# One ring and one DMA queue for K, V and weights, and identity matmuls in place of an add tree, in a decode step

## The chip, the cores and the metric

The kernel runs on one core of one Trainium2 chip. The metric is the time of one execution on the device in microseconds (us). The kernel before takes 1370.1 us (median of 3 runs, 1369.82 to 1370.17). All times named "span" run from the first to the last instruction of a profiled execution and are about 2 to 3 us shorter than the measured time.

## The reference, cut to what matters

One token (a row x of 640 values) goes through attention over a cache and through a gated FFN. The results and x are added up.

```python
xn = layernorm(x)                                   # 1 x 640
q  = xn @ wq                                        # 32 heads x 128
scores = einsum("hd,hkd->hk", q, k_cache) * 128**-0.5   # 32 heads, 32768 keys
p  = softmax(scores)
o  = einsum("hk,hkd->hd", p, v_cache)
y  = x + o.reshape(4096) @ wo + (silu(xn @ w_gate) * (xn @ w_up)) @ w_down
```

The K cache and the V cache have 32 heads x 32768 keys x 128 values in bf16, 268 MB each. With the weights some 555 MB have to come from HBM. One head has 16.78 MB of K and V.

## The kernel before

K lies in SBUF with 128 keys on the partitions and the 128 values of a key along the free axis. So the dot product with q is a multiply and a sum along the free axis, and both are VectorE's. V needs no such work: TensorE takes blocks of V as stationary operand and a column of p as moving operand (the PV matmuls, below).

K has its own ring of four slots of 2 MB, loaded from SyncE's queue. V has another ring of four, loaded from ScalarE's queue. A head has four K chunks. VectorE's loop, cut:

```python
for i in range(NKC):                  # NKC = 128 chunks of 2 MB
    h, c = divmod(i, NCK)             # NCK = 4 chunks per head
    ...
    v.wait_ge(kdma[slot].sem, ...)    # chunk landed
    dve_t.inc(v.tensor_tensor(out=kr, in0=kr, in1=qbh, op=ALU.mult))
    for w in [64, 32, 16, 8]:         # the add tree, in place
        dve_t.inc(v.tensor_tensor(out=kr[:, :, 0:w], in0=kr[:, :, 0:w],
                                  in1=kr[:, :, w:2 * w], op=ALU.add))
    v3 = dve_t.inc(v.tensor_reduce(out=scs[...], in_=kr[:, :, 0:8], axis=AX.X, op=ALU.add))
    ...
    if c == NCK - 1:
        head_ops(h)                   # max over the free axis: pmax
        if h >= 1:
            rz_op(h - 1)              # waits for GpSimd's sum of head h-1, then 1/sum
```

GpSimd joins the partitions, and ScalarE makes the exp between GpSimd's two steps:

```python
for b in range(H):                                  # GpSimd
    wait(pmax of b);  partition_all_reduce(gmaxb, pmax, max)
    tensor_scalar(negb = -scale * gmaxb)            # ScalarE: exp waits for this
    wait(exp of b);   partition_all_reduce(zb, rowsum, add)   # rz_op waits for this
```

Of the kernel before, what the change touches and what calls it, by code (L numbers as in the profile page):

```python
# [5 lines left out]
ALU = mybir.AluOpType  # L7
# [4 lines left out]


class Ctr:

    def __init__(self, sem, step=1):
        self.sem = sem
        self.step = step
        self.n = 0

    def inc(self, ins):
        ins.then_inc(self.sem, self.step)
        self.n += self.step
        return self.n


def bass_parallel_sum__gqa_block_cached__swiglu_ffn__decode_kernel(
# [16 lines left out]
    HQ = A_wq.shape[1] // DH  # L44
    F = B_w_gate.shape[1]
    assert DH == 128 and HQ == H, (DH, HQ, H)
    assert D % 128 == 0
    NC_D = D // 128
    NJ = SK // 128
    assert SK % 128 == 0  # L50
    CKK = 64 if NJ >= 64 else NJ
    CKV = 64 if NJ >= 64 else NJ
    assert NJ % CKK == 0 and NJ % CKV == 0
    NCK = NJ // CKK
    NCV = NJ // CKV
    NKC = NCK * H
    NVC = NCV * H
    KR = 4
    VR = 4
    PR = 3  # L60
    SCR = 3
    SR = 4
    TREE = [64, 32, 16, 8]
    NLVL = 2 + len(TREE)
    c_scale = float(DH) ** -0.5
    eps = 1e-5
    FB = (F + 127) // 128
    F_LAST = F - (FB - 1) * 128
    DB = 2
    DBW = D // DB  # L70
    QB = min(512, HQ * DH)
    NQB = (HQ * DH) // QB
    assert D % DB == 0 and DBW <= 512 and (HQ * DH) % QB == 0

    VPK = NCV // NCK
    order = []
    emitted_v = set()

    def _emit_v(q):
        if 0 <= q < NVC and q not in emitted_v:  # L80
            order.append(("v", q))
            emitted_v.add(q)

    for i in range(NKC):
        order.append(("k", i))
        h = i // NCK
        ci = i % NCK
        for vv in range(VPK):
            _emit_v((h - 1) * NCV + ci * VPK + vv)
    for q in range(NVC):  # L90
        _emit_v(q)
    assert CKV == CKK, "V-in-K-slot staging needs equal chunk sizes"
    LASTV_Q0 = (H - 1) * NCV

    def v_buf(q):
        return ("v", q % VR, None)
    WO_POS = min(KR - 1, NKC - 1)
    FFNW_POS = min(1, NKC - 1)

    with ExitStack() as es:  # L100
# [5 lines left out]

        krings = sbt("krings", [128, KR, CKK * DH], BF16)
        vrings = sbt("vrings", [128, VR, CKV * DH], BF16)
        WQO = max(NC_D * HQ * DH, H * D)
        wqo = sbt("wqo", [128, WQO], BF16)  # L110
        qb = sbt("qb", [128, HQ * DH], BF16)
        xnb = sbt("xnb", [128, NC_D, 128], BF16)
        sc = sbt("sc", [128, SCR, NJ], F32)
        P = sbt("P", [128, PR, NJ], BF16)
        ocol = sbt("ocol", [128, HQ], BF16)
        xncol = sbt("xncol", [128, NC_D], BF16)
        hcol = sbt("hcol", [128, FB], BF16)
        sg = sbt("sg", [128, FB], F32)
        pmax = sbt("pmax", [128, SR], F32)
        gmaxb = sbt("gmaxb", [128, SR], F32)  # L120
        negb = sbt("negb", [128, SR], F32)
        rowsum = sbt("rowsum", [128, SR], F32)
        zb = sbt("zb", [128, SR], F32)
        rzb = sbt("rzb", [128, SR], F32)
        xrowb = sbt("xrowb", [1, D], BF16)
        rows = sbt("rows", [1, 4, D], F32)
        outb = sbt("outb", [1, D], BF16)
        st = sbt("st", [1, 8], F32)
        one1 = sbt("one1", [1, 2], F32)
        s_x = sem("c_x")  # L130
        s_wq = sem("c_wq")
        s_ffn = sem("c_ffn")
        s_wo = sem("c_wo")
        s_out = sem("c_out")
        kd_sems = [sem(f"kd{i}") for i in range(KR)]
        vd_sems = [sem(f"vd{i}") for i in range(VR)]
        s_pe_a = sem("pe_a")
        s_pe_pv = sem("pe_pv")
        s_pe_c = sem("pe_c")
        s_dve_a = sem("dve_a")  # L140
        s_dve_t = sem("dve_t")
        s_dve_max = sem("dve_max")
        s_dve_rz = sem("dve_rz")
        s_dve_c = sem("dve_c")
        s_act_a = sem("act_a")
        s_act_exp = sem("act_exp")
        s_act_ov = sem("act_ov")
        s_pool_a = sem("pool_a")
        s_pool_g = sem("pool_g")
        s_pool_neg = sem("pool_neg")  # L150
        s_pool_z = sem("pool_z")
        block = es.enter_context(nc.Block())

        c_x = Ctr(s_x, 16)
        c_wq = Ctr(s_wq, 16)
        c_ffn = Ctr(s_ffn, 16)
        c_wo = Ctr(s_wo, 16)
        c_out = Ctr(s_out, 16)
        kdma = [Ctr(s, 16) for s in kd_sems]
        vdma = [Ctr(s, 16) for s in vd_sems]  # L160
        pe_a = Ctr(s_pe_a)
        pe_pv = Ctr(s_pe_pv)
        pe_c = Ctr(s_pe_c)
        dve_a = Ctr(s_dve_a)
        dve_t = Ctr(s_dve_t)
        dve_max = Ctr(s_dve_max)
        dve_rz = Ctr(s_dve_rz)
        dve_c = Ctr(s_dve_c)
        act_a = Ctr(s_act_a)
        act_exp = Ctr(s_act_exp)  # L170
        act_ov = Ctr(s_act_ov)
        pool_a = Ctr(s_pool_a)
        pool_g = Ctr(s_pool_g)
        pool_neg = Ctr(s_pool_neg)
        pool_z = Ctr(s_pool_z)

        kflat = krings[:, :, :].rearrange("p s n -> p (s n)")
        vflat = vrings[:, :, :].rearrange("p s n -> p (s n)")
        wq_v = wqo[:, 0:NC_D * HQ * DH].rearrange("p (c n) -> p c n", c=NC_D)
        wo_v = wqo[:, 0:H * D].rearrange("p (h n) -> p h n", h=H)  # L180
        assert 2 * NC_D * F + FB * D <= VR * CKV * DH, "V ring too small to host FFN weights"
        wg_sb = vflat[:, 0:NC_D * F].rearrange("p (c n) -> p c n", c=NC_D)
        wu_sb = vflat[:, NC_D * F:2 * NC_D * F].rearrange("p (c n) -> p c n", c=NC_D)
        wd_sb = vflat[:, 2 * NC_D * F:2 * NC_D * F + FB * D].rearrange("p (j d) -> p j d", j=FB)
        VSLOTS_FFN = ((2 * NC_D * F + FB * D) * 2 + CKV * DH * 2 - 1) // (CKV * DH * 2)
        xf = rows[0:1, 0, :]
        xc = rows[0:1, 1, :]
        xnrow = rows[0:1, 2, :]
        ffnrow = rows[0:1, 3, :]
        mile = {}  # L190

        with nc.psum_tensor("ps8", [128, 8, 512], F32) as ps8:
            psA = ps8[:, 0, :]
            psG = ps8[:, 1, :]
            psF = ps8[0:1, 2:2 + DB, :]
            psR = ps8[0:1, 4:6, :]
            O = [ps8[:, 6, :], ps8[:, 7, :]]
            QPS = [ps8[:, b, 0:QB] for b in range(8)]
            assert NQB <= 8

            @block.vector
            def dve_phase_a(v):
                dve_a.inc(v.memset(one1[0:1, :], 1.0))
                v.wait_ge(c_x.sem, 16)
                dve_a.inc(v.tensor_copy(out=xf, in_=xrowb[0:1, :]))
                v.wait_ge(dve_a.sem, dve_a.n)
                dve_a.inc(v.tensor_reduce(out=st[0:1, 0:1], in_=xf, axis=AX.X, op=ALU.add))
                v.wait_ge(dve_a.sem, dve_a.n)
                dve_a.inc(v.tensor_scalar(out=st[0:1, 1:2], in0=st[0:1, 0:1], scalar1=1.0 / D,
                                          scalar2=None, op0=ALU.mult))  # L210
                v.wait_ge(dve_a.sem, dve_a.n)
                dve_a.inc(v.tensor_scalar(out=xc, in0=xf, scalar1=st[0:1, 1:2], scalar2=None,
                                          op0=ALU.subtract))
                v.wait_ge(dve_a.sem, dve_a.n)
                dve_a.inc(v.tensor_tensor_reduce(out=xnrow, in0=xc, in1=xc, scale=1.0, scalar=0.0,
                                                 op0=ALU.mult, op1=ALU.add, accum_out=st[0:1, 2:3]))
                v.wait_ge(dve_a.sem, dve_a.n)
                mile["ve"] = dve_a.inc(v.tensor_scalar(out=st[0:1, 3:4], in0=st[0:1, 2:3], scalar1=1.0 / D,
                                                       scalar2=eps, op0=ALU.mult, op1=ALU.add))

            @block.scalar
            def act_phase_a(a):
                a.wait_ge(dve_a.sem, mile["ve"])
                mile["sqrt"] = act_a.inc(a.activation(out=st[0:1, 4:5], in_=st[0:1, 3:4], func=ACTF.Sqrt))

            @block.vector
            def dve_phase_a2(v):
                v.wait_ge(act_a.sem, mile["sqrt"])
                dve_a.inc(v.reciprocal(out=st[0:1, 5:6], in_=st[0:1, 4:5]))
                v.wait_ge(dve_a.sem, dve_a.n)  # L230
                mile["xnrow"] = dve_a.inc(v.tensor_scalar(out=xnrow, in0=xc, scalar1=st[0:1, 5:6],
                                                          scalar2=None, op0=ALU.mult))
# [104 lines left out]
            def dve_phase_b(v):  # L337
# [14 lines left out]
                for i in range(NKC):  # L352
# [4 lines left out]
                    if c == 0 and h >= SCR:  # L357
                        v.wait_ge(act_exp.sem, h - SCR + 1)
# [195 lines left out]
```

## Time and profile before

| | |
|---|---|
| span | 1367.0 us |
| VectorE busy | 1263.9 us, 92% |
| bytes moved | 555.19 MB, 406 GB/s over the span |
| VectorE per 2 MB of K | 9.82 us from chunk to chunk |
| from one head's max to the next (mean of heads 4 to 29) | 39.80 us |

First come lines of the page of the kernel before: the busy time of the engines, then three rows of 40 equal slices of the span (busy tenths of VectorE, busy tenths of the DMA engines, GB/s), then the chain that ended last, by engine.

```profile
PE 272.6 (20%) x8474; PEld 240.2 (18%) x8474; DVE 1263.9 (92%) x859; ACT 31.9 (2%) x102; POOL 201.3 (15%) x100
...
DVE  5907999999999999999999999999999999999994
...
DMA  9999599999999999999999999999999999999994
GB/s 389 401 415 381 214 424 388 419 419 415 416 426 418 427 418 422 424 419 426 418 421 420 424 420 423 427 420 425 422 421 424 417 427 425 419 426 427 414 381 183
...
DVE 90%; another core or an unknown queue 3%; issue 2%; SPq 2%; DMA 1%; PE 1%; POOL 0%; ACT 0%; POOLq 0%
```

VectorE is full except at the start and the end, and it is the chain. But the DMA row is full as well, at 414 to 427 GB/s from the eighth slice to the third from the end. The fifth slice moves only 214 GB/s and the last only 183.

The groups of instructions by shape say what a chunk costs VectorE (count, then busy us and mean ns of one, then idle time before them):

```profile
L361 DVE TENSOR_TENSOR krings<-krings,qb 128x8192 bf16<-128x8192 bf16 x128 | 564.9, 4413 | 43.5 <-DMA krings<-in_A_k_cache_dram 43.5
L365 DVE TENSOR_TENSOR krings<-krings 128x4096 bf16<-128x4096 bf16 x128 | 293.3, 2292 | 4.4
...
L365 DVE TENSOR_TENSOR krings<-krings 128x2048 bf16<-128x2048 bf16 x128 | 156.8, 1225 | 4.4
...
L365 DVE TENSOR_TENSOR krings<-krings 128x1024 bf16<-128x1024 bf16 x128 | 88.5, 691 | 4.4
L368 DVE TENSOR_REDUCE sc<-krings 128x64 f32<-128x512 bf16 x128 | 87.8, 686 | 4.4
L365 DVE TENSOR_TENSOR krings<-krings 128x512 bf16<-128x512 bf16 x128 | 54.3, 424 | 4.4
```

The multiply takes 4.41 us and the four steps of the tree 2.29, 1.23, 0.69 and 0.42 us, together 4.63 us.

### The profile page before, as it was taken

Reading aid. Unit: us, or ns where it says so; the run is one execution under the profiler, and the core shown is the slowest. Engines: PE = TensorE matmul, PEld = TensorE weight load, DVE = VectorE, ACT = ScalarE, POOL = GpSimd, SP = SyncE. Lnnn points to the kernel's source line nnn. Section 1 sums busy time; section 2 is a strip of 40 time slices with the busy share of each in tenths; the row PEclk is TensorE's granted clock in tenths of the full one; section 3 lists DMA queues with packets and bytes.
Section 4 is the critical chain, followed back from the end, with each engine's and each line's share of the span. In section 5 each row is a group of like instructions: output and inputs, shape, how many; then the busy total and the mean of one; then the engine's idle time right before and its main releaser. Section 6 shows DMA issues by size and latency. Waiting matters only on the chain.

```text
span 1367.0 us, 18528 instructions
## 1 busy us (share of the span) xinstructions
PE 272.6 (20%) x8474; PEld 240.2 (18%) x8474; DVE 1263.9 (92%) x859; ACT 31.9 (2%) x102; POOL 201.3 (15%) x100
## 2 busy tenths in 40 slices
PE   3320102222111222211122221112222111222222
PEld 1220102222101222210122221112222111222222
DVE  5907999999999999999999999999999999999994
ACT  0000000000000000000000000000000000000000
POOL 0000222111111211111121111111111111110120
PEclk9555555555555555555555555555555555555555
DMA  9999599999999999999999999999999999999994
GB/s 389 401 415 381 214 424 388 419 419 415 416 426 418 427 418 422 424 419 426 418 421 420 424 420 423 427 420 425 422 421 424 417 427 425 419 426 427 414 381 183
DMA packets 44850, 555.19 MB, mean 406 GB/s; under 512 B 4258, under 2 KB 10084, under 8 KB 11364
## 3 DMA queue, kind: packets, MB, share of 16 engines
q1 hardware_dynamic: 26340, 285.57, 50.4%
q10 hardware_dynamic: 18432, 268.44, 46.5%
q8 instruction: 66, 1.08, 0.3%
q14 instruction: 12, 0.10, 0.0%
HBM read 553.99 MB, written 0.00 MB: 405 GB/s over the span
## 4 chain that ended last, share of the span: by engine, by line
DVE 90%; another core or an unknown queue 3%; issue 2%; SPq 2%; DMA 1%; PE 1%; POOL 0%; ACT 0%; POOLq 0%
DVE krings L365 43%; DVE krings L361 40%; DVE sc L368 6%; DMA vrings<-in_B_w_down_dram 1%; SPq L499 1%; PE ps L466 1%; SPq L498 0%; DVE rzb L349 0%; PE ps L287 0%; SPq L494 0%; DVE pmax L343 0%; PE ps L440 0%; SPq L513 0%; DVE rows L483 0%
## 5 line engine op out<-in xcount | busy, mean ns | idle before, releaser
L365 DVE TENSOR_TENSOR krings<-krings 128x4096 bf16<-128x4096 bf16 (+3 forms) x512 | 592.9, 1158 | 17.5
L361 DVE TENSOR_TENSOR krings<-krings,qb 128x8192 bf16<-128x8192 bf16 x128 | 564.9, 4413 | 43.5 <-DMA krings<-in_A_k_cache_dram 43.5
L466 PE MATMUL ps<-P,vrings 128*128 128x1 bf16 x8192 | 229.5, 165 | 209.0 <-ACT P L424 105.5
L466 PEld LDWEIGHTS ps<-P,vrings 128*128 128x128 bf16 x8192 | 223.9, 104 | 228.4 <-ACT P L424 105.8
L387 POOL PARTITION_ALL_REDUCE gmaxb<-pmax x32 | 136.3, 4259 | 542.6 <-DVE pmax L343 542.6
L440 PE MATMUL ps<-wqo,ocol 128*1 128x320 bf16 x64 | 22.0, 449 | 850.7 <-ACT P L424 850.7
L440 PEld LDWEIGHTS ps<-wqo,ocol 128*1 128x1 bf16 x64 | 2.8, 81 | 853.6 <-ACT P L424 853.2
L368 DVE TENSOR_REDUCE sc<-krings 128x64 f32<-128x512 bf16 x128 | 87.8, 686 | 4.4
L394 POOL PARTITION_ALL_REDUCE zb<-rowsum x32 | 40.3, 1258 | 265.2 <-issue 265.2
L390 POOL TENSOR_SCALAR negb<-gmaxb 128x1 f32<-128x1 f32 x32 | 24.6, 767 | 351.4 <-issue 351.4
L424 ACT ACTIVATE P<-sc,negb 128x256 bf16<-128x256 f32 x32 | 16.3, 508 | 917.1 <-POOL negb L390 917.1
L349 DVE RECIPROCAL rzb<-zb 128x1 f32<-128x1 f32 x32 | 4.9, 153 | 14.4 <-POOL zb L394 14.4
L414 ACT ACTIVATE ocol<-ps,rzb 128x1 bf16<-128x1 f32 x32 | 8.4, 263 | 360.4 <-PE ps L466 360.4
L274 DVE CAST qb<-ps 128x512 bf16<-128x512 f32 x8 | 5.5, 692 | 11.9 <-PE ps L264 11.9
L343 DVE TENSOR_REDUCE pmax<-sc 128x1 f32<-128x256 f32 x32 | 13.4, 419 | 1.1
L264 PE MATMUL ps<-wqo,xnb 128*128 128x512 bf16 x40 | 10.1, 418 | 7.6 <-DMA wqo<-in_A_wq_dram 7.6
L287 PE MATMUL ps<-xncol,vrings 128*128 128x1 bf16 (+1 forms) x140 | 4.4, 168 | 16.7 <-DMA vrings<-in_B_w_down_dram 16.7
L287 PEld LDWEIGHTS ps<-xncol,vrings 128*128 128x128 bf16 (+1 forms) x140 | 4.3, 108 | 17.2 <-DMA vrings<-in_B_w_down_dram 17.2
L328 PE MATMUL ps<-vrings,hcol 128*1 128x320 bf16 (+1 forms) x28 | 6.4, 400 | 0.8 <-DVE hcol L307 0.8
L264 PEld LDWEIGHTS ps<-wqo,xnb 128*128 128x128 bf16 x40 | 4.2, 106 | 13.2 <-issue 9.5
L424 ACT ACTIVATION_READ_ACCUMULATOR P<-sc,negb 128x1 f32 x32 | 6.0, 187 | 0.0
L328 PEld LDWEIGHTS ps<-vrings,hcol 128*1 128x1 bf16 (+1 forms) x28 | 2.8, 104 | 4.4 <-issue 1.1
(31 smaller groups left out, 17.1 us busy)
## 6 DMA issues: line engine op xcount, KB each, us to landing
krings<-in_A_k_cache_dram SPq DMA_DIRECT2D x128, 2048.0 KB, 17.1
vrings<-in_A_v_cache_dram ACTq DMA_DIRECT2D x128, 2048.0 KB, 26.1
wqo<-in_A_wq_dram SPq DMA_DIRECT2D x5, 1024.0 KB, 9.0
wqo<-in_A_wo_dram SPq DMA_DIRECT2D x1, 5120.0 KB, 71.2
vrings<-in_B_w_gate_dram SPq DMA_DIRECT2D x1, 2160.0 KB, 26.4
vrings<-in_B_w_up_dram SPq DMA_DIRECT2D x1, 2160.0 KB, 31.1
vrings<-in_B_w_down_dram SPq DMA_DIRECT2D x1, 2080.0 KB, 31.7
vrings<-in_B_w_down_dram SPq DMA_DIRECT2D x1, 80.0 KB, 18.1
```

Source lines behind the costliest of these rows:

```text
L264: mm = t.matmul(QPS[b], lhsT=xnb[:, c, :], rhs=wq_v[:, c, b * QB:(b + 1) * QB], start=(c == 0), stop=(c == NC_D - 1))
L343: v1 = dve_max.inc(v.tensor_reduce(out=pmax[:, b % SR:b % SR + 1], in_=scs, axis=AX.X, op=ALU.max))
L361: dve_t.inc(v.tensor_tensor(out=kr, in0=kr, in1=qbh[:, None, :].to_broadcast([128, CKK, DH]), op=ALU.mult))
L365: dve_t.inc(v.tensor_tensor(out=kr[:, :, 0:w], in0=kr[:, :, 0:w], in1=kr[:, :, w:2 * w], op=ALU.add))
L368: v3 = dve_t.inc(v.tensor_reduce(out=scs[:, c * CKK:(c + 1) * CKK], in_=kr[:, :, 0:TREE[-1]], axis=AX.X, op=ALU.add))
L387: v1 = pool_g.inc(g.partition_all_reduce(gmaxb[:, s:s + 1], pmax[:, s:s + 1], channels=128, reduce_op=ReduceOp.max))
L390: v2 = pool_neg.inc(g.tensor_scalar(out=negb[:, s:s + 1], in0=gmaxb[:, s:s + 1], scalar1=-c_scale, scalar2=None, op0=ALU.mult))
L394: v3 = pool_z.inc(g.partition_all_reduce(zb[:, s:s + 1], rowsum[:, s:s + 1], channels=128, reduce_op=ReduceOp.add))
L424: v1 = act_exp.inc(a.activation(out=P[:, b % PR, :], in_=sc[:, b % SCR, :], func=ACTF.Exp, bias=negb[:, b % SR:b % SR + 1], scale=c_scale, ...
L440: mm = t.matmul(psR[0:1, b, 0:DBW], lhsT=ocol[:, h:h + 1], rhs=wo_v[:, h, b * DBW:(b + 1) * DBW], start=(h == 0), stop=(h == H - 1))
L466: mm = t.matmul(ob[:, 0:1], lhsT=ring[:, vslot, jj * DH:(jj + 1) * DH], rhs=P[:, pslot, j:j + 1], start=(j == 0), stop=(j == NJ - 1))
L499: c_ffn.inc(sp.dma_start(wd_sb[:, 0:FB - 1, :], B_w_down[0:(FB - 1) * 128, :].rearrange("(j p) n -> p j n", p=128)))
```

## The change

Its intent is to take VectorE off the critical path, and to keep the DMA engines busy from the first microsecond to the last. The add tree goes: after the multiply, 16 matmuls with a 128x128 identity as stationary operand add 16 groups of 8 columns into one PSUM bank (the folds, below), and VectorE only reduces the last 8 to 1. K, V and all weights pass through one ring of five slots of 4 MB, and all loads go through SyncE's queue in one fixed order: K of head h, V of head h-1, in turns. Each load of K or V is contiguous in HBM. The order of the instructions in the loops was written anew. The core of the diff:

```diff
-        krings = sbt("krings", [128, KR, CKK * DH], BF16)     # 4 x 2 MB
-        vrings = sbt("vrings", [128, VR, CKV * DH], BF16)     # 4 x 2 MB
+        ring = sbt("ring", [128, NS, CW], BF16)               # 5 x 4 MB
...
+    for h in range(H):
+        for c in range(NCH):                                  # NCH = 2 chunks per head
+            stream.append(("k", h, c, 0, JC))
+            if h:
+                stream.append(("v", h - 1, c, 0, JC))
+    stream.append(("o", 0, 0, 0, 0))                          # output weights, two halves
+    stream.append(("o", 1, 0, 0, 0))
+    ...                                                       # V of the last head
...  VectorE, for each K chunk of 4 MB:
-                    for w in TREE:
-                        ... add ...
+                    for s in range(SPC):                      # SPC = 2 halves of 2 MB
+                        v.tensor_tensor(out=kr, in0=kr, in1=qh, op=ALU.mult).then_inc(s_mul, 1)
+                    for s in range(SPC):
+                        v.wait_ge(s_fold, m + 1)
+                        v.tensor_reduce(out=sc[...], in_=fold[m % 2]..., op=ALU.add).then_inc(s_red, 1)
+                    if c == 0 and h:
+                        recip(h - 1)
+                    if c == NCH - 1:
+                        ... max: pmax ...
-                    if c == NCK - 1:
-                        head_ops(h)
-                        if h >= 1:
-                            rz_op(h - 1)
...  TensorE:
+                            for f in range(NF):               # NF = 16
+                                mm = t.matmul(fold[m % 2]..., lhsT=ident[:, :],
+                                              rhs=kr[:, :, f * DS:(f + 1) * DS],
+                                              start=(f == 0), stop=(f == NF - 1))
```

## The prediction

> **What bounds the kernel now.** VectorE is busy 1263.9 of 1367.0 us (92%) and holds 90% of the chain that ended last. A 2 MB K chunk costs it 4.41 us of multiply, an add tree of 2.29 + 1.23 + 0.69 + 0.42 us and a reduce of 0.69 us (groups by shape): 9.82 us from chunk to chunk in the timeline, 9.96 with the per-head operations. With V that is 4.19 MB in 9.96 us = 421 GB/s. The windows show a DMA share of 1.00 at 421 to 423 GB/s there, so the second bound, HBM traffic, stands only 1 to 3% behind; the tree is not worth its busy time.
>
> Outside the steady stretch DMA time is lost. At 68.8 to 112.3 us VectorE waits 43.5 us for K behind V bursts and the 5 MB output weights; then, at 130 to 169 us, only 219 GB/s move, as V slots wait for that late head's exp: about 19 us lost against 425 GB/s. In the last 32 us 167 GB/s move (K's tree, max, GpSimd, exp and PV follow): another 19 us.
>
> **What the change does.** It removes the tree (4.6 us per 2 MB) and adds, per 2 MB, 16 identity matmuls of 512 columns and a reduce out of PSUM. Here 128x512 matmuls paced 0.43 us at first and 0.216 us at full clock: 3.5 to 6.8 us per fold. A PSUM read of 512 fp32 took 0.69 us (the cast of q). Per K+V pair of 8.4 MB (19.5 us at 430 GB/s): VectorE 2 x (4.41 + 0.69) = 10.2 us; TensorE 7 to 13.7 us of folds plus 128 PV matmuls at 27.3 ns = 3.5 us. Both fit, even at half clock. VectorE falls to about 670 us busy; TensorE rises to 700 to 1100 us (estimates). A K slot comes free 13 to 17 us after landing, with four chunks of 9.8 us queued behind it: no starvation. exp follows the max by 15 us here; V arrives one pair later, which covers it.
>
> **So DMA bounds it after.** Bytes stay 555 MB. Attainable: 431 to 433 GB/s at 10 to 20 us (one queue), 429 at 175 to 200 us (K plus a V burst). The Trainium skill, "DMA: Bandwidth & Descriptors", section Bandwidth, gives 425 GB/s for a 16 MB load and a port ceiling of 435; this trace lies between. One queue instead of two should not matter (same page, "Issuing engines are not separate DMA queues"). At 430 GB/s (estimate): 1291 us, plus 2 us before the first bytes, 4 after the last, 3 between span and time: about **1300 us**. Of the 70 us gained some 25 come from the rate, 19 from the start-up hole, 15 from the tail, the rest from the start.
>
> **Range:** 1286 to 1320. Faster by over 2%: 0.91; within 2%: 0.06; slower by over 2%: 0.03.
>
> **What would show it:** DMA row at 9 throughout, 425 to 433 GB/s, no hole in the fifth slice; VectorE near 50%, waiting for DMA before each multiply; fold pace 0.22 to 0.43 us; the chain made of DMA landings; last landing to end below 7 us.
>
> **What would make it wrong:** the folds read 16 bytes every 256 bytes; at half rate a fold would take up to 13.7 us and TensorE would bind near 1900 us. If slots come free late (fold behind PV, late exp) the single queue runs dry and stops K as well as V. If 4 MB chunks draw less than 425 GB/s, the time is over 1313 us.

## More of the kernel before

The timeline of one head shows where the reciprocal stands (start, duration, engine, line, operation):

```profile
606.82 0.51 ACT L424 ACTIVATE P<-sc,negb 128x256 bf16<-128x256 f32 x1 [27.99 <-POOL negb L390]
...
615.17 1.44 POOL L394 PARTITION_ALL_REDUCE zb<-rowsum  x1 [8.39 <-issue]
...
629.36 0.42 DVE L343 TENSOR_REDUCE pmax<-sc 128x1 f32<-128x256 f32 x1
629.70 0.15 DVE L349 RECIPROCAL rzb<-zb 128x1 f32<-128x1 f32 x1
```

The exp starts at 606.82 us and the sum over partitions is there at 616.6 us. The reciprocal that needs the sum comes at 629.70 us, 13 us later, and has not waited (a wait would be shown in brackets at the end of the line).

## The result, and the profile after

The kernel after takes 1379.06 us (median of 4 runs, 1375.61 to 1381.83); before takes 1370.13 us in the same rounds. The ratio is 1.006 (95% interval 1.0045 to 1.0077). Every ratio in this document is the mean time of one kernel's runs over that of the other's of the same rounds, so it is not quite the ratio of the medians that are quoted. The predicted 1300 us, and a gain of 70 us, did not come.

The same lines of the page of the kernel after:

```profile
PE 826.3 (60%) x10524; PEld 462.5 (34%) x10524; DVE 669.9 (49%) x342; ACT 34.4 (3%) x107; POOL 160.4 (12%) x102
...
DVE  2554555453565343555344653535654445653542
...
DMA  9999999999999999999999999999999999999994
GB/s 383 429 429 428 432 422 432 429 423 401 410 409 422 407 424 382 401 408 404 413 418 383 389 381 399 425 408 401 409 406 416 430 398 402 380 399 411 422 380 195
...
issue 48%; PE 22%; DVE 13%; POOL 12%; SPq 2%; ACT 1%; DMA 1%; POOLq 0%; ACTq 0%; DVEq 0%
```

VectorE fell to 669.9 us busy, where 670 was predicted. TensorE rose to 826.3 us, within 700 to 1100. The holes at the start and at the end are smaller. But from the tenth slice to the last but one the rate lies between 380 and 430 GB/s where before it was 414 or more up to the last two slices, while the DMA row still shows 9: in tenths of busy time a queue that runs nearly dry once per head can't be seen. In windows of 3 us it can. Here are two of them, one head apart (the last two numbers are the DMA share and GB/s):

```profile
603.00:606.00 3.00, 3.00 (x51) 1.91 (x50) 0.79 (x2) 0.00 (x0) 0.00 (x0) 1.00 0.56 240
645.00:648.00 3.00, 3.00 (x87) 2.41 (x86) 1.78 (x3) 0.00 (x0) 0.57 (x1) 1.00 0.81 257
```

Between 400 and 1200 us a single load of K or V was in flight for 26% of the time and two for 69%; in run e1 below there were never fewer than three (worked out from the traces).

And the chain is no longer VectorE's and not DMA's either: 48% of it is "issue", that is, time in which the engine waited for nothing that the profile shows.

Who waited for whom, VectorE's two longest waits for something other than the folds (total us, times, longest):

```profile
DVE rz L285 <- POOL zb L233: 402.8, 32, 18.5
...
DVE ring L295 <- DMA ring<-in_A_k_cache_dram: 13.5, 1, 13.5
```

VectorE waits for a K load once, for 13.5 us at the start. It waits for GpSimd's sum in every head, 402.8 us in all or 12.6 us per head. The chain of waits, in order of time, from one head's max to the next head's max (start, duration, what):

```profile
605.90 0.43 DVE pmax L309
...
606.42 4.46 POOL gmax L227
...
610.94 10.99 issue
621.93 0.27 POOL neg L230
...
622.29 0.61 ACT P L340 x2
622.90 9.14 issue
632.04 0.41 POOL zb L233
...
632.47 0.16 DVE rz L285
632.64 4.33 DVE ring L295
...
637.01 9.14 PE ps L410 x32
...
646.18 0.70 DVE sc L302
...
646.91 0.43 DVE pmax L309
```

This is a closed ring of waits, which has nothing to do with the ring of slots. The max (605.90) starts GpSimd's all-reduce; 10.99 us of "issue" pass; then scaling and exp follow; another 9.14 us of "issue" pass; GpSimd's sum (632.04) lets VectorE take the reciprocal (632.47). Only then can VectorE go on to the multiply of the head's second K chunk, whose fold, reduce and max start the next turn. One turn takes 41.01 us here, and 41.49 us on average over heads 4 to 29. At 430 GB/s the 16.78 MB of a head need 39.0 us.

What closes the ring is one place in the program. In the kernel before `rz_op(h - 1)` stands after the last chunk of head h, a whole head after the max that its sum comes from. Here `recip(h - 1)` stands after the first of the two chunks of head h.

### The profile page after: what moved, and what is told of

Its sections match the earlier page's. It is cut to its first block, busy times and chain, and to the rows that moved or that the text cites. A ratio compares the mean times of both kernels' runs of the same rounds, so it can differ in the third digit from the quotient of the medians.

```text
span 1376.4 us, 22157 instructions
## 1 busy us (share of the span) xinstructions
PE 826.3 (60%) x10524; PEld 462.5 (34%) x10524; DVE 669.9 (49%) x342; ACT 34.4 (3%) x107; POOL 160.4 (12%) x102
## 4 chain that ended last, share of the span: by engine, by line
issue 48%; PE 22%; DVE 13%; POOL 12%; SPq 2%; ACT 1%; DMA 1%; POOLq 0%; ACTq 0%; DVEq 0%
PE ps L410 22%; DVE ring L295 10%; POOL gmax L227 10%; DVE sc L302 2%; SPq L207 1%; ACT P L340 1%; DMA ring<-in_A_k_cache_dram 1%; DVE pmax L309 1%; POOL zb L233 1%; POOL neg L230 1%; PE ps L422 0%; DVE rz L285 0%; SPq L202 0%; POOLq L230 0%; PE ps L396 0%
## 5 line engine op out<-in xcount | busy, mean ns | idle before, releaser
L410 PE MATMUL ps<-ring,ident 128*128 128x512 bf16 x2048 | 578.2, 453 | 423.7 <-DVE ring L295 423.7
L295 DVE TENSOR_TENSOR ring<-ring,qb 128x8192 bf16<-128x8192 bf16 x128 | 559.7, 4414 | 13.5 <-DMA ring<-in_A_k_cache_dram 13.5
L410 PEld LDWEIGHTS ps<-ring,ident 128*128 128x128 bf16 x2048 | 226.1, 113 | 750.8 <-DVE ring L295 421.6
L422 PE MATMUL ps<-P,ring 128*128 128x1 bf16 x8192 | 219.7, 164 | 106.8 <-ACT P L340 106.8
L422 PEld LDWEIGHTS ps<-P,ring 128*128 128x128 bf16 x8192 | 217.3, 99 | 129.5 <-ACT P L340 122.2
L302 DVE TENSOR_REDUCE sc<-ps 128x64 f32<-128x512 f32 x128 | 88.5, 692 | 262.6 <-PE ps L410 262.6
L285 DVE RECIPROCAL rz<-zb 128x1 f32<-128x1 f32 x32 | 5.2, 164 | 402.8 <-POOL zb L233 402.8
L227 POOL PARTITION_ALL_REDUCE gmax<-pmax x32 | 138.5, 4329 | 526.2 <-DVE pmax L309 526.2
L233 POOL PARTITION_ALL_REDUCE zb<-rsum x32 | 12.8, 401 | 316.9 <-issue 316.9
L340 ACT ACTIVATE P<-sc,neg 128x256 bf16<-128x256 f32 x32 | 16.2, 508 | 482.3 <-POOL neg L230 482.3
L396 PE MATMUL ps<-ring,ocol 128*1 128x320 bf16 x64 | 10.5, 329 | 0.4 <-ACT ocol L331 0.4
L269 DVE CAST qb<-ps 128x512 bf16<-128x512 f32 x4 | 2.5, 684 | 10.6 <-PE ps L361 10.6
```

The lines of the kernel that those rows point to most:

```text
L227: g.partition_all_reduce(gmax[:, s:s + 1], pmax[:, s:s + 1], channels=128, reduce_op=RO.max).then_inc(s_g, 1)
L233: g.partition_all_reduce(zb[:, s:s + 1], rsum[:, s:s + 1], channels=128, reduce_op=RO.add).then_inc(s_z, 1)
L295: v.tensor_tensor(out=kr, in0=kr, in1=qh, op=ALU.mult).then_inc(s_mul, 1)
L302: v.tensor_reduce(out=sc[:, h % NB, o:o + JS], in_=fold[m % 2].rearrange("p (j d) -> p j d", d=DS), axis=AX.X, op=ALU.add).then_inc(s_red, 1)
L340: a.activation(out=P[:, h % NB, :], in_=sc[:, h % NB, :], func=ACTF.Exp, bias=neg[:, h % NR:h % NR + 1], scale=c_scale, accum_out=rsum[:, ...
L396: m_ = t.matmul(psR[0:1, b, 0:DW], lhsT=ocol[:, h:h + 1], rhs=w_[:, h % HP, b * DW:(b + 1) * DW], start=False, stop=(h == H - 1))
```

## The experiments

The theory is: (L) this ring of latencies, closed by the early reciprocal, sets the time. The rivals are: (1) one queue with 4 MB chunks draws only the 404 GB/s that the page shows; (2) TensorE's folds, at a clock that is granted at 0.73 of full speed, are the bound.

### e1: the reciprocal later; e2: the sum without GpSimd

```diff
 # e1
-                    if c == 0 and h:
-                        recip(h - 1)
                     if c == NCH - 1:
                         ... max: pmax ...
+                        if h:
+                            recip(h - 1)
 # e2 (the reciprocal stays early)
-  GpSimd: wait(exp of h); partition_all_reduce(zb, rsum, add)
+  TensorE, before PV of head h: matmul(ps[:, h % 2, 0:1], lhsT=ones128x128, rhs=rsum[:, h])
```

> The kernel after, with one instruction moved: VectorE's reciprocal of head h-1 stands after the max of head h, not between the two K chunks of head h. Theory (a loop of latencies): per head the max, GpSimd's all-reduce, exp, GpSimd's second all-reduce, the reciprocal, then the second chunk's multiply, fold and max form a ring of 41.4 us, longer than the 39.0 us that 16.8 MB take at 430 GB/s; moved, the reciprocal waits for nothing, the ring falls to about 30 us and DMA binds: 1290 to 1312 us, 425 GB/s or more in the steady stretch. Rival 1 (one queue with 4 MB chunks draws only 403 to 407 GB/s): unchanged, 1370 to 1385 us. Rival 2 (the folds on a TensorE at partial clock bind): unchanged too, as TensorE's work is the same.

> The kernel after with the reciprocal left where it is, but the sum over partitions made by a 128x128 matmul with ones instead of GpSimd's second all-reduce (9.2 us from exp to its end). Theory (loop): the ring loses about 8 us, 41.4 to 33 us, less than DMA's 39.0, so DMA binds: 1290 to 1315 us. Rivals 1 and 2: unchanged at 1370 to 1385 us (TensorE has even a little more to do).

Measured: e1 takes 1323.12 us (1322.39 to 1324.39), ratio 0.966 to before. e2 takes 1321.98 us (1321.58 to 1322.19), ratio 0.965. Two different edits that open the same ring give the same time, with the same loads, the same queue and the same folds. That rules out both rivals as causes of the 1379 us. In e1 VectorE now waits for loads, as was predicted of the kernel after, and the reciprocal waits once, at the very end:

```profile
DVE ring L295 <- DMA ring<-in_A_k_cache_dram: 323.4, 61, 13.7
...
DVE rz L285 <- POOL zb L233: 21.5, 1, 21.5
```

The page of e1 shows the rate and the chain, which is now made of K loads:

```profile
GB/s 379 430 433 428 423 427 426 425 431 432 425 429 426 426 429 426 432 426 429 427 429 426 429 423 432 430 428 425 429 424 431 429 425 425 427 426 420 428 303 306
...
DMA 67%; PE 21%; DVE 8%; SPq 4%; issue 0%; ACT 0%; DVEq 0%
```

But both runs missed the expected time: e1 came out 11 us over the end of its range, e2 7 us. Part of the prediction is still wrong in e1; the runs from e9 on are about that.

### e3 and e4: the sum done twice

```diff
+                    g.partition_all_reduce(zb, rsum, add).then_inc(s_z0, 1); g.wait_ge(s_z0, h + 1)
                     g.partition_all_reduce(zb, rsum, add).then_inc(s_z, 1)
```

> The kernel after with GpSimd's second all-reduce done twice: the dose doubled. Theory (loop): each of some 31 heads grows by one all-reduce, 5 to 9 us: 1540 to 1680 us, with the same DMA work and the same folds. Rivals 1 and 2: GpSimd is only 12% busy, so at most 1% more.

> The same doubled all-reduce, in the kernel with the reciprocal moved. Theory (loop): off the ring there, so within 2% of e1 (GpSimd itself then needs some 35 us per head, just under 39). If instead GpSimd's work is dear wherever the reciprocal stands, it costs here what it costs in e3.

Measured: e3 takes 1401.33 us (two runs; ratio 1.023 to before), e4 1322.41 us. The expected size was wrong, because the second all-reduce in a row is not a second dose of 5 to 9 us. The timeline of GpSimd in e3:

```profile
628.62 0.26 POOL L231 TENSOR_SCALAR neg<-gmax 128x1 f32<-128x1 f32 x1 [10.81 <-issue]
640.21 0.40 POOL L234 PARTITION_ALL_REDUCE zb<-rsum  x1 [11.34 <-issue]
640.72 0.38 POOL L237 PARTITION_ALL_REDUCE zb<-rsum  x1
```

The sum starts 11.3 us after the scaling ended (with the exp between), but its repetition is done 0.5 us after it. What is long is not the all-reduce itself but the change between an all-reduce and the other kind of operation, in both directions: 10.81 us stand before the scaling, which follows an all-reduce, and 11.34 us before the sum, which follows the scaling. (The profile's spans on GpSimd are rough, so how these times split between two neighbours is not certain.) What remains of the test still agrees with the theory: where the added operation is in the ring, heads follow in 42.06 us instead of 41.49. That is 0.57 us more, about the length of the added operation, and over 32 heads 18 of the 22 us by which e3 is slower than the kernel after. Where it is not in the ring it costs nothing (e4 against e1).

### e5 and e6: the same reciprocal in the kernel before

```diff
-                        if h >= 1:
-                            rz_op(h - 1)              # after chunk 3
+                    if c == 0 and h >= 1:             # e5; e6: c == 2
+                        rz_op(h - 1)
```

> The kernel before, with its reciprocal of head h-1 moved from the end of head h to after the first of head h's four K chunks. Theory (a wait that stands too early in an in-order engine): in the trace of before the sum comes back 26.9 us after the max (17.2 to exp, 9.7 on to the sum), the first chunk ends 9.8 us after it, so VectorE stalls 12 to 17 us per head: 1740 to 1900 us. Rival (the loss belongs to the new ring, queue or folds): the old kernel has none of them, so within 1% of before.

> The same reciprocal after the third of four chunks, 29.5 us after the max, later than the 26.9 us that the sum takes: no stall, within 1% of before by the theory and by the rival.

Measured: e5 takes 1688.12 us (ratio 1.232), e6 1370.95 us (ratio 1.001). The position of one instruction of 0.15 us costs the old kernel 318 us. The waits of e5:

```profile
DVE rzb L349 <- POOL zb L394: 329.0, 31, 13.9
```

The 329 us of that wait cover the whole loss. The stall was 10.6 us per head and not 12 to 17, because the sum came back 20.8 us after the max and not 26.9. Why GpSimd was quicker is not shown: in e5 VectorE stood still for part of that time, and the DMA engines moved 333 GB/s instead of 422 (from 400 to 1200 us). So the early reciprocal needs neither the new ring nor the folds to do harm.

### e7: the new ring with the old tree

```diff
-  TensorE: 16 identity matmuls per half;  VectorE: tensor_reduce out of PSUM
+  VectorE: four tensor_tensor adds in place, tensor_reduce of 8 columns (as before)
```

This is e1 (late reciprocal) with the tree.

> e1 with VectorE's add tree back in place of the identity matmuls: the new ring, queue, chunks and start alone. e1's heads follow each other in 39.73 us (loads land at the pace of the slowest DMA engine), the tree needs 4 x 9.82 + 0.55 = 39.84 us per head, so the steady stretch is the same and only the end is later: 1328 to 1342 us against e1's 1323. If, as predicted, taking away the tree were worth 430 against 421 GB/s (25 us), it would be 1348 us or more.

Measured: 1342.70 us (1341.76 to 1343.92), ratio 0.980, just over the end of the expected range. Heads follow in 39.80 us, in e1 in 39.73 us. So of e1's gain of 46 us over before, some 27 come from the ring of slots, the queue and the order of the loads, and some 20 from the folds, but hardly any of these from the steady stretch: 0.07 us per head make 2 us.

The expectation put the difference to e1 at the end. The traces put it at the start. e7 reaches the max of head 4 at 242.3 us and the kernel before at 271.1 us, which is already the whole gain of e7; from the last max to the end of the span e7 needs 22.6 us and the kernel before 20.8. e1 reaches the max of head 4 at 216.4 us, another 26 us earlier: its first max comes 10 us sooner, and the next four heads follow in 35.8 us each, where VectorE with the tree needs 39.8 for each. At the end e1 loses some 10 us of this again. It needs 32.7 us from the last max to the end, because its last V load lands only at 1317.4 us.

### e8 and e12: the output weights elsewhere

In e1 a row of 33.3 us on SyncE's timeline covers the issue of the two loads of the output weights, whose rows have 1280 bytes, and the windows show 222 and 103 GB/s at 1275 to 1285 us. The expectation of e8 takes the row for one time of issuing, and that is a misreading: the row merges two issues, which took 0.38 and 16.51 us, with 16.4 us between them in which SyncE waited for a free slot. The view by line tells them apart (shortest, median and longest in ns, first and last start in us):

```profile
L212 SPq DMA_DIRECT2D ring<-in_A_wo_dram x2: 379/8444/16510, 1250.6 to 1267.4; - x2
```

e8 issues these loads from ScalarE's queue. e12 gives them a buffer of their own (and the ring four slots), and loads them in eight pieces between heads 5 and 26.

> e1 with the two loads of the output weights (rows of 1280 bytes) issued from ScalarE's queue, not in line between K and V on SyncE's. In e1 SyncE is held 33.3 us by these two issues and the DMA falls to 222 and 103 GB/s at 1275 to 1285 us. If holding the only queue is what costs there: 9 to 14 us less than e1, 1309 to 1314 us, no hole. If the small rows themselves are what is slow: within 4 us of e1.

> e1 with the output weights in a buffer of their own, loaded in eight pieces of 640 KB between the K and V loads of heads 5 to 26, and four ring slots instead of five. In e1 and e8 these 1280-byte rows stand near the end and hold up what follows: DMA at 222 and 103 GB/s. Early they hide in the stream: 9 to 14 us less than e1, 1309 to 1314 us, no hole at the end. If four slots are too few, heads take longer than 39.8 us.

Measured: e8 takes 1334.45 us and e12 1327.31 us, both slower than e1. The expectation was wrong for both. The timeline of e8 at the end:

```profile
1250.54 42.27 SPq L214 DMA_DIRECT2D ring<-in_A_v_cache_dram  x5
...
1268.79 37.96 ACTq L350 DMA_DIRECT2D ring<-in_A_wo_dram  x1
...
1313.92 6.20 PEld L404 LDWEIGHTS ps<-ring,ocol 128*1 128x1 bf16 x32 [19.31 <-DMA ring<-in_A_wo_dram]
```

The first row is merged too. SyncE's V issues are short, and the rest of the 42.27 us is waiting for free slots:

```profile
L214 SPq DMA_DIRECT2D ring<-in_A_v_cache_dram x66: 327/328/442, 40.4 to 1292.4; - x66
```

So SyncE was freed, and ScalarE's queue is held instead, for 37.96 us by the second load. But the output weights land 49.4 and 51.8 us after their issue, in e1 40.2 and 30.5, and TensorE, which takes them before the last V, gets to them only at 1313.92 us.

In e12 heads follow in 40.26 us instead of 39.73: the 5.24 MB cost their time (12.2 us at 428 GB/s) inside the stream instead of at its end. The four slots are a rival, as e12's expectation says, but they cost little: the 22 heads up to head 26 take 40.33 us each (13 us more than in e1 in all), and the five after the last piece 39.68, in e1 39.63. It ends with exp at 1314.51 us and the PV after it. e12 has no hole before the last slice of its page and gained nothing by that, so the hole in e1 was hardly a loss. The next runs show what was one.

### e9, e10, e11: what keeps e1 from 1300 us

The trace records when each of the 16 DMA engines reports its share of a load. Sorted, relative to the first engine, in us, for the load that completed nearest to 1105 us (worked out from the trace, which here does not name the engines):

```
after   0.0  0.1  0.1  0.2  0.3  0.3  0.4  0.5  0.6  1.3  1.4  1.5  1.6  1.6  1.8  2.0
e1      0.0  0.3  0.4  1.1 12.1 12.3 12.4 12.6 12.8 12.8 14.1 14.2 19.3 21.3 21.4 23.3
e9      0.0  0.2  0.5  0.7  2.9  3.0  4.8  4.9  5.0  5.1  5.3  5.6 19.6 20.6 21.6 22.4
e10     0.0  0.0  0.2  0.2  0.2  0.7  0.9  3.0 12.5 12.6 12.7 12.8 14.0 14.2 14.3 14.8
e13     0.0  0.1  0.3  0.9 12.3 12.3 12.5 12.8 12.9 14.1 14.2 14.4 19.0 20.5 20.9 21.9
e14     0.0  0.2  0.3  0.4  0.5  0.9  1.0  3.3  3.3  4.8  5.0  5.2  5.2  5.2  5.3  5.4
e15     0.0  0.2  0.4  0.4  0.5  1.1  1.3  3.3 12.6 12.6 12.8 14.1 14.1 14.3 14.3 14.7
```

In e1 the queue never runs dry, and the engines drift apart over a thousand microseconds (the last one is 4.1 us behind the first at 200 us, 8.1 at 400 and 14.4 at 700): four are ahead, eight are some 13 us behind them, four some 21 us. A chunk can be used when its last share has landed, so the slowest engines set the pace. 16.78 MB in 39.73 us are 422 GB/s, while the windows, which average over the engines, show 427. It may also explain part of the hole at the end, where the fast engines run out of work before the slow ones: in e14 below, where all finish within 5.4 us, the last two slices of the page have 401 and 327 GB/s, in e1 303 and 306. That engines of a group in one run are those of the same group in another is read from the sizes of the groups, four and eight; the trace does not show it. The Trainium skill, "Perfetto Trace Analysis", section What "DMA-bound" means, lists "Specific DMA engines" as the first of three possible bounds; this trace agrees, with 21 us of drift.

The edits: e9 does only every eighth PV matmul (`range(j0, j1, 8)`), which takes away 14,336 instructions. e10 takes all all-reduces out of GpSimd (the sum as in e2, the bias of exp 0 instead of the max). e11 reads K and V with the layout of before.

> e1 with one of eight PV matmuls only (wrong result on purpose; same loads, 14,336 instructions fewer). In e1 the 16 DMA engines drift apart: the last engine's share of a K load lands 23 us after the first's at 1100 us, and heads follow in 39.73 us although 428 GB/s move (39.2 us). If the fetches of instructions (83 of 16 KB) burden some engines: spread below 10 us at 1100 us, heads at about 39.2 us, 1304 to 1312 us. If not: spread above 18 us and within 4 us of e1's 1323.

> e1 without any GpSimd all-reduce: the sum by a matmul with ones as in e2, and exp with a bias of 0 instead of the max (these scores are small, so the result stays right). The chain from max to sum loses its 20 us. Theory: e1 is bound by the slowest DMA engine's landings, not by that chain any more, so nothing in the steady stretch: heads at 39.7 us and within 4 us of e1. If GpSimd's work is what slows some DMA engines: spread below 10 us and 1304 to 1312 us.

> e1 with K and V read as the kernel before reads them (a partition's rows 64 KB apart) in the same 4 MB loads of 32 KB rows, not from one contiguous 4 MB. Both theories of the loss say nothing of it: within 3 us of e1. If contiguity is worth something: slower than e1 by 10 us or more.

Measured: e9 1322.62 us, e10 1313.11 us (ratio 0.959), e11 1322.47 us. Contiguity is worth nothing here (e11 against e1's 1323.12). In e9 the eight middle engines caught up to within 6 us of the first, but the last four did not, and so the time did not move. In e10 the last four caught up, eight stayed 12 to 15 us behind, and heads follow in 39.38 us. So e10's expectation by the theory ("nothing in the steady stretch") was wrong, and each of the two suspects burdens its own group of engines. (e9, and e14 below, were meant to give a wrong result; both were accepted by the comparison with the reference all the same. They are experiments, not versions.)

### e13, e14, e15: the two burdens apart and together

e13 is e10 with GpSimd doing all its operations per head on a constant tile, and nobody waiting for them. e14 is e10 with every eighth PV matmul only. e15 is meant for use: the max over partitions comes from TensorE too.

```diff
 # e15, per head
+  TensorE: matmul(row[1,128],   lhsT=pmax[:, h],        rhs=identity_fp32)
+  VectorE: tensor_reduce(gm[1,1], row, max)
+  TensorE: matmul(col[128,1],   lhsT=row_of_minus_scale, rhs=gm)
+  VectorE: tensor_copy(neg[:, h], col)
-  GpSimd:  both all-reduces and the scaling
```

> e10 (1313 us) with GpSimd doing the two all-reduces and the scaling per head as e1 does, at the same triggers, on a constant tile, and nobody reading or awaiting them. If the all-reduces burden some DMA engines by themselves: back to e1, 1320 to 1325 us, the last engine 20 us or more behind the first at 1100 us. If it was the chain from max to exp that cost: as e10, 1311 to 1315 us, 15 us behind.

> e10 with one of eight PV matmuls only (wrong result on purpose): neither all-reduces nor most of the instruction fetches. If these two are what sets the slow engines apart: all 16 within 7 us at 1100 us, heads every 38.9 to 39.1 us (a 32 KB packet takes 1.213 us, 432 GB/s over 16 engines), 1301 to 1307 us. If a third cause stands behind them: within 3 us of e10's 1313.

> A version meant to be used: e2's sum and e1's reciprocal, and the max over partitions by TensorE (a matmul with an fp32 identity turns the column to a row, VectorE reduces it, a matmul with a row of -scale spreads it), so that GpSimd does nothing in the loop and the softmax stays as it was. If e10's gain comes from idle GpSimd: 1311 to 1316 us, correct. If the added round trips between VectorE and TensorE (some 3 us per head, with 10 us of slack on both) show: above 1320 us.

Measured: e13 1323.31 us, e14 1301.57 us (1301.51 to 1301.71), e15 1313.07 us (1312.94 to 1313.17), ratios 0.966, 0.950 and 0.958 to before.

e13 puts the 10 us back although nothing waits for GpSimd, and its last four engines are 19 to 22 us behind again. So GpSimd's operations by themselves (per head two all-reduces and the scaling) slow some DMA engines. Two things narrow this down. e2 had no all-reduce for the sum any more, and its last four engines were 20 to 23 us behind all the same: the max's all-reduce and the scaling are enough. And K and V come in packets of 32 KB that mostly take 1.213 us. Between 112 and 1105 us 173 of them took more than 1.5 us in e13, and 68 in e10. Of the 173, 147 began in the intervals, some half of the time, in which GpSimd shows nothing before the scaling or the sum (worked out from the traces).

e14 takes both burdens away: all 16 engines within 5.4 us, heads in 39.01 us, 1301.6 us. The windows from 400 to 1200 us (columns: busy us and count of PE, PEld, DVE, ACT, POOL; then granted clock, DMA share, GB/s) of before, after, e1 and e14, in this order:

```profile
400.00:1200.00 800.00, 156.41 (x5160) 141.89 (x5160) 785.60 (x523) 17.31 (x60) 128.87 (x60) 0.50 1.00 422
```

```profile
400.00:1200.00 800.00, 473.81 (x6109) 264.91 (x6106) 400.01 (x193) 16.69 (x58) 100.05 (x58) 0.73 0.96 404
```

```profile
400.00:1200.00 800.00, 498.01 (x6403) 278.54 (x6404) 420.73 (x202) 17.30 (x60) 51.97 (x60) 0.72 1.00 427
```

```profile
400.00:1200.00 800.00, 396.43 (x2010) 173.71 (x2008) 426.55 (x207) 15.70 (x63) 0.00 (x0) 0.72 1.00 431
```

VectorE goes from 785.6 us busy in 800 to 400.0 and 420.7, and yet the rate falls from 422 to 404 GB/s in the kernel after; e1 has 427 and e14 431. The queue of instruction fetches moved 1.36 MB in e1 and 0.44 MB in e14 (packets, MB, share):

```profile
q8 instruction: 83, 1.36, 0.4%
```

```profile
q8 instruction: 27, 0.44, 0.1%
```

The edit takes away matmuls and their fetches together, so that the fetches, and not the matmuls themselves, hold back the eight engines is the likely reading and was not tested apart. An estimate from the traces speaks for it: up to 1105 us the fetch packets took 73.8 us in e10 and 24.6 us in e14. Spread over eight engines that is 9.2 and 3.1 us for each, of the 12.5 to 14.8 us and 3.3 to 5.4 us by which these eight were behind. How fetches and GpSimd's operations reach the DMA engines is not shown by these runs either. The Trainium skill, "Runtime: NRT & Kernel Launch", section Instruction fetch mechanics, says that instructions are fetched over DMA in blocks of 16 KiB, which the 83 packets of 16 KB in e1 agree with, and that crossing a block is mostly hidden; the PV matmuls with their fetches, together with GpSimd's burden, cost 21.5 us here (e1 against e14). For GpSimd see the last section.

e15 beats both kernels with the softmax as it was, by 4.2% against before.

## Why the prediction was wrong, point by point

- **What bounds the kernel before**: right. VectorE binds at 39.8 us per head and DMA stands close behind. As far as e1's loads tell, it stands even closer than the "1 to 3%" of the prediction: at 39.7 us per head in e1, with GpSimd and the fetches as they are.
- **The costs of the change**: right. The multiply stayed at 4.41 us and the reduce out of PSUM took 0.69 us. Reading 16 bytes every 256 cost the folds nothing: 32 matmuls in 8.4 to 10.0 us, at 0.43 us for the first and 0.21 to 0.22 us for the later ones. VectorE was predicted at 670 us busy and has 669.9.
- **"exp follows the max by 15 us here; V arrives one pair later, which covers it."** This is the step that failed. It followed the head's chain from the max to exp and to V, and stopped there. The chain goes on, through GpSimd's sum (10.55 us after exp on average) to a reciprocal on VectorE, and the diff puts that reciprocal between the two K chunks of the next head. VectorE waited there 12.6 us per head, and the ring became 41.49 us long. Moving that one instruction took the time from 1379 to 1323 us (e1), opening the ring elsewhere did the same (e2), and closing such a ring in the old kernel cost it 318 us (e5).
- **"A K slot comes free 13 to 17 us after landing … no starvation"**: wrong for the same reason. The slots were freed late because the multiply started late: in the kernel after it starts 18.1 us after the landing of a head's first chunk and 25.5 us after that of the second, and the folds end 31.6 and 39.0 us after the landing (means). In e1 it starts at the landing, and the folds end 13.7 us after it, as predicted. The prediction did name "slots come free late" as a danger, but looked for it at TensorE and exp.
- **"DMA row at 9 throughout"**: it came true and proved nothing; the DMA row is at 9 at 404 GB/s too.
- **"At 430 GB/s"**: mis-sized for this kernel by 22 us. The rate was read in windows of 10 to 25 us, as a mean over the 16 engines. Over a thousand microseconds the slowest four engines set the pace, at 422 GB/s. GpSimd's all-reduces with the scaling cost 10 us of the difference (e1 to e10, confirmed by e13) and the PV matmuls, likely by their instruction fetches, 11.5 us more once those are gone (e10 to e14). With both gone heads take 39.01 us, 430 GB/s, and the time is 1301.6 us.
- **One queue "should not matter"**: right. e1 draws more on one queue than the kernel before on two. Contiguous chunks, of which the prediction says nothing, did not matter either: e11 is as fast as e1. The Trainium skill, "DMA: Bandwidth & Descriptors", section "Issuing engines are not separate DMA queues", agrees with it on the queue.
- **The gain at the start and end**: right for the start, too large for the end. The ring with the tree and a late reciprocal gains 27 us (e7), all of it by the max of head 4 (28.8 us), where 19 us and something from the start were predicted. Of the 15 us from the tail e7 shows nothing, and in e1, where the loads bind, the DMA engines lose 12.5 us against 425 GB/s in the last 40 us, before 20.0 (worked out from the traces): 7.5 us gained.

The steps add up: 1379 us measured, less 56 (ring of waits, e1), less 10 (GpSimd, e10), less 11.5 (PV matmuls with their fetches, e14) makes 1301.6. They do so by construction, since each is the difference of two runs. That e14 comes next to the predicted 1300 us says that the predicted rate can be reached, but e14 leaves out seven of eight PV matmuls and the max, so it does not make the prediction right for the kernel that was changed.

What stays open: which DMA engines are slow, whether the fetches or the matmuls themselves hold eight of them back, by what path GpSimd loads them, and what GpSimd does in the 9 to 11 us before the scaling and before the sum.

## What to carry to other kernels

When a change shortens an engine's work, follow each dependency chain all the way around to where it re-enters an in-order engine, and check for every wait how long after its producer it stands: a reciprocal of 0.16 us can carry the time. Where the DMA row reads full, divide bytes by time per turn of the loop before you believe that DMA binds; and where it does bind, look at how far apart the engines finish, because the slowest one is the bound and not their mean (here 422 and 427 GB/s). Work that seems to have nothing to do with the loads, such as GpSimd's all-reduces here, can slow some of these engines only.

## What the Trainium skill lacked or had wrong

- "GPSIMD Engine Reference", section Instruction dispatch, says that the first call to a freshly loaded kernel takes a code load of about 6 us that no instruction shows. Here invisible time came back in every head, twice, at each change between an all-reduce and the scaling: 10.99 us before the scaling and 9.14 us before the sum in one turn of the kernel after, against 0.5 us for an all-reduce directly behind another (e3). The page does not say that this can recur; that it is such a load is likely but not shown.
- No page says that GpSimd's all-reduces (with the scaling between them) slow a part of the 16 DMA engines: with them (e13) the last four engines were 19 to 22 us behind at 1105 us, without them (e10) the last was 15 us behind; 10 us of 1323.
- "Runtime: NRT & Kernel Launch", section Instruction fetch mechanics, calls crossing a block "mostly hidden". In a kernel bound by DMA it may cost time all the same: 14,336 PV matmul instructions and 56 fetch packets fewer gave 11.5 us (e10 to e14), and the eight engines that had been behind came within 5.4 us; while GpSimd's burden was there, the same edit gave 0.5 us (e1 to e9). That this is the fetches' doing is likely but was not separated from the matmuls.
- "DMA: Bandwidth & Descriptors", section Bandwidth, gives one rate for a load of a given size and does not say how far the engines can finish apart (elsewhere the page does call two of them usually slower). Here twelve of 16 fell behind, by 12 to 23 us at 1105 us; the mean over the engines was 427 GB/s and the usable rate 422 (e1).
